# The last 64 tokens' mixing of a token mixer, written as products on half of TensorE's array

## The chip, the cores and the metric

The kernel runs on one core of a Trainium2 chip. The metric is the device time of one execution in microseconds; three executions of the kernel before gave 269.45, 269.69 and 269.77 us, a median of 269.69. The engines are called TensorE (PE in the profile, with PEld for its weight loads), VectorE (DVE), ScalarE (ACT), GpSimd (POOL) and SyncE (SP, which issues most of the transfers here).

## The reference

Eight batches; each is a linear attention of 8 heads over 576 tokens with head size 64, followed by an MLP mixer over 512 features. Written per batch:

```
phi(x)  = concat(relu(x) * cos_w, relu(x) * sin_w)      # [576, 128] per head
kv      = phi(k)^T @ v            ; z = sum over tokens of phi(k)
x       = (phi(q) @ kv) / (phi(q) @ z + 1e-6)           # heads side by side: [576, 512]
h       = relu(x^T @ w_tok1) @ w_tok2                   # token mixing: 576 -> 256 -> 576
u       = x + h^T
out     = u + relu(u @ w_ch1) @ w_ch2                   # channel mixing: 512 -> 1536 -> 512
```

Inputs and outputs are float32; the products take bfloat16 operands and add up in float32.

## The kernel before, in words

576 tokens are 4 x 128 + 64. The 512 "main" tokens of a batch are cut into four chunks of 128 (R = 4 chunks; chunk number ci is 0 to 3), and the last 64 tokens are a fifth chunk, numbered R. Two batches, an even one and the odd one after it, share the tiles of the last tokens: the even batch has partitions 0 to 63 and the odd one 64 to 127 (`half(0)` and `half(1)`; `self.rows` is the batch's own half). So the features of q and k, their transposes and the channel mixing of the last tokens are worked for two batches at once.

The token mixing of the last tokens is not shared. It runs once per batch on whole-array products in which half of the rows or half of the results go to nothing:

- `num` (L353 to L371) makes one chunk of x: 8 products, one per head, of 65 columns (64 values and the denominator), then a reciprocal and a multiplication on VectorE. For chunk R the stationary operand is the shared transposed q of both batches, so 128 result rows come out, and VectorE keeps only the batch's own 64 of them. x of the last tokens is kept in a tile of 128 rows whose other half was cleared to zero once at the start (L162 to L164).
- `tok1` (L373 to L383) is the first token mixing, 576 tokens to 256: for each of the two blocks of 128 hidden tokens (mi) it adds up five products of 512 columns, one per chunk, in the order `ORDER = (0, 1, 2, R, 3)`. For chunk R the weights stand in both halves of `w_tail1`, and the zero rows of x make the other half add nothing. `tok1_out` (L385) applies relu and stores B1.
- `tok2` (L391 to L413) is the second token mixing, 256 to 576: two products of 512 columns per chunk (ki), an addition of x on VectorE that gives u, and a cast on ScalarE. For chunk R the weights' 64 columns stand twice, so that the result comes out on both halves, and VectorE adds x on the batch's own 64 rows only.

After that, u is transposed by a DMA (for chunk R once per pair), and the channel mixing (`Channel`, L532 to L634) runs: `c_main` 12 x 4 products of 512 columns, `o_step` 12 products of 512 columns per chunk, and in odd batches the same for the shared last tokens.

The order of all this is written out by hand. The program of each batch's channel mixing is a list of steps (`Channel.steps`), and the preparation of the next batch, from features to token mixing, is put behind numbered steps of it by the table in `Front.pieces` (L461 to L527). There, C counts from the first c step and O from the first o step; `(t + at, T, ci)` places the second token mixing, `mix` the first, `N` the numerators. A batch's token mixing thus falls between the o steps of the batch before. The lines of that table that place the mixing:

```python
plan += [(mix, self.mix_head, 0), (mix + 1, self.mix_head, 1),
         (mix + 2, self.mix_tail)]
plan += [(t + at, T, ci) for ci, at in enumerate((0, 1, 2, 3, 3) if not first else
                                                 (0, 0, 1, 2, 2))]
```

`mix_head` does chunks 0, 1, 2 and R of one block, `mix_tail` chunk 3 and the relu. The first batch has no batch before it and is prepared by `first_front` (L636 to L712), in which the denominators are made separately (`dens`, L295); its u of chunk R is made at step 10 of its own channel mixing and cast at step O + 8 (L477, L483).

SyncE's queue holds the loads of q, k and v, the transposing DMAs and the stores; POOL's queue holds the weight loads (L182 to L198).

Of the kernel before, what the change touches and what calls it, by code (L numbers as in the profile page):

```python
# [9 lines left out]
F32 = mybir.dt.float32  # L10
BF16 = mybir.dt.bfloat16
# [5 lines left out]
def kernel(  # L17
# [15 lines left out]
    nc = tc.nc  # L33

    B, H, S, D = q.shape
    F = 2 * D
    Dm = H * D
    S_tok, D_tok = moe_w_tok1.shape
    Dm2, D_ch = moe_w_ch1.shape
    P = 128  # L40
    R = S // P
    SM = R * P
    ST = S - SM
    NSC = R + 1
    NCC = Dm // P
    NT = D_tok // P
    NCH = D_ch // P
    HH = H // 2
    D1 = D + 1
    DP = 80  # L50
# [2 lines left out]


    ORDER = (0, 1, 2, R, 3)

    def half(g):
        return slice(g * ST, (g + 1) * ST)
# [7 lines left out]
    twos = ctx.enter_context(tc.tile_pool(name="twos", bufs=2))  # L66
    o_out = ctx.enter_context(tc.tile_pool(name="o_out", bufs=4))
    phi = ctx.enter_context(tc.tile_pool(name="phi", bufs=R))
    once = ctx.enter_context(tc.tile_pool(name="once", bufs=1))
    const = ctx.enter_context(tc.tile_pool(name="const", bufs=1))  # L70
    small = ctx.enter_context(tc.tile_pool(name="small", bufs=4))
    ps_mm = ctx.enter_context(tc.tile_pool(name="ps_mm", bufs=4, space=bass.MemoryType.PSUM))
# [44 lines left out]
    w_tok2n = stage2[:, 0:NT * S].rearrange("p (n s) -> p n s", n=NT)  # L117
# [7 lines left out]
    w_ch2 = const.tile([P, NCH, Dm], BF16, name="w_ch2")  # L125
    w_tok1 = const.tile([P, R, D_tok], BF16, name="w_tok1")

    w_tail1 = const.tile([P, D_tok], BF16, name="w_tail1")
    w_tok2 = const.tile([P, NT, SM + P], BF16, name="w_tok2")
    ident = head.tile([P, P], BF16, name="ident")  # L130
    make_identity(nc, ident)
    pos_i = head.tile([P, NSC], mybir.dt.int32, name="pos_i")
# [19 lines left out]
    nc.gpsimd.memset(ones[half(1), 1:2], 0.0)  # L152


    v_augs, x_tails = [], []
    for i in range(2):
        va = const.tile([P, NSC, H, DP], BF16, name=f"v_aug{i}")
        nc.vector.memset(va[:, 0:R, :, D:D1], 1.0)
        nc.vector.memset(va[half(1 - i), R, :, :], 0.0)
        nc.vector.memset(va[half(i), R, :, D:D1], 1.0)  # L160
        v_augs.append(va)
        xt = const.tile([P, Dm], BF16, name=f"x_tail{i}")  # L162
        nc.vector.memset(xt[half(1 - i), :], 0.0)
        x_tails.append(xt)  # L164

    class Tail:

# [12 lines left out]
    for t in (tail0.kp, tail0.qp):  # L180
        nc.gpsimd.memset(t[half(1)], 0.0)
    for g in range(2):  # L182
        nc.gpsimd.dma_start(out=w_tail1[half(g), :], in_=moe_w_tok1[SM:S, :])
    C2 = D_ch // 2
    w_ch1_done = []
    for c2 in range(2):
        for ki in range(0, NCC, 2):
            w_ch1_done.append(nc.gpsimd.dma_start(
                out=w_ch1[:, ki:ki + 2, c2 * C2:(c2 + 1) * C2],
                in_=moe_w_ch1[ki * P:(ki + 2) * P, c2 * C2:(c2 + 1) * C2]  # L190
# [18 lines left out]
    def permute_tok2(ki):  # L209
        nc.scalar.copy(w_tok2[:, ki, 0:SM].rearrange("t (r p) -> t r p", r=R),  # L210
                       w_tok2n[:, ki, 0:SM].rearrange("t (p r) -> t r p", r=R))
        nc.scalar.copy(w_tok2[:, ki, SM:].rearrange("t (g s) -> t g s", g=2),
                       w_tok2n[:, ki, None, SM:S].to_broadcast([P, 2, ST]))


    class Front:
# [17 lines left out]
        def q_of(self, ci):  # L234
            return self.qp[ci] if ci < R else self.tail.qp

        def qT_of(self, ci, h):
            return self.qpT[:, ci * H + h, :] if ci < R else self.tail.qpT[:, h, :]

        def x_of(self, ci):  # L240
            return self.x[:, ci, :] if ci < R else self.xt

        def rows_of(self, ci):
            return slice(0, P) if ci < R else self.rows

        def feature(self, which, ci, j, heads=(0, H), on_act=False):
            lo, hi = heads
# [18 lines left out]
        def values(self, ci, eng, heads=(0, H)):  # L266
            lo, hi = heads
            if ci < R:
                src = self.vt[:, lo:hi, ci * D:(ci + 1) * D]
            else:  # L270
                src = self.tail.vt[self.rows, lo:hi, :]
            dst = self.va[self.rows_of(ci), ci, lo:hi, 0:D]
            if eng is nc.scalar:
                nc.scalar.copy(dst, src)  # L274
            else:
                eng.tensor_copy(dst, src)
# [18 lines left out]
        def dens(self, ci):  # L295

            if ci == 0:
                self.d_ps = ps_mm.tile([P, NSC * H], F32, name="d_ps", tag="mm")
                self.d_sb = small.tile([P, NSC * H, 1], F32, name="d_sb")
            for h in range(H):  # L300
                i = ci * H + h
                nc.tensor.matmul(self.d_ps[:, i:i + 1], self.qT_of(ci, h),  # L302
                                 self.ks_sb[:, h:h + 1], start=True, stop=True)

        def dens_out(self, lo, hi):
            nc.vector.tensor_scalar_add(self.d_sb[:, lo:hi, 0], self.d_ps[:, lo:hi], 1e-6)
# [46 lines left out]
        def num(self, ci, fill=0, dens=False):  # L353
            num_ps = ps_at.tile([P, 2, 512], F32, name="num_ps", tag="at")
            if fill:
                busy(num_ps[:, 0, HH * DP:512], 1)
            for h in range(H):
                g, j = divmod(h, HH)
                nc.tensor.matmul(num_ps[:, g, j * DP:j * DP + D1], self.qT_of(ci, h),  # L359
                                 self.kv_sb[g][:, j, 0:D1], start=True, stop=True)  # L360
            rows = self.rows_of(ci)
            nv = num_ps[rows, :, 0:HH * DP].rearrange("p g (j d) -> p g j d", d=DP)
            if dens:
                den = self.d_sb[rows, ci * H:(ci + 1) * H, :].rearrange("p (g j) o -> p g j o", g=2)
            else:
                den = small.tile([P, 2, HH, 1], F32, name="den")[rows]
                nc.vector.tensor_scalar_add(den, nv[:, :, :, D:D1], 1e-6)
                nc.vector.reciprocal(den, den)
            nc.vector.tensor_mul(  # L369
                self.x_of(ci)[rows].rearrange("p (g j d) -> p g j d", g=2, j=HH),  # L370
                nv[:, :, :, 0:D], den.to_broadcast([rows.stop - rows.start, 2, HH, D]))  # L371

        def tok1(self, mi, chunks):  # L373
            if not hasattr(self, "B1"):
                self.B1 = once.tile([P, NT, Dm], BF16, name="B1")
                self.b1_ps = {}
            if mi not in self.b1_ps:
                self.b1_ps[mi] = ps_mm.tile([P, Dm], F32, name="b1_ps", tag="mm")
            cols = slice(mi * P, (mi + 1) * P)
            for ci in chunks:  # L380
                w = w_tok1[:, ci, cols] if ci < R else w_tail1[:, cols]
                nc.tensor.matmul(self.b1_ps[mi], w, self.x_of(ci),  # L382
                                 start=(ci == ORDER[0]), stop=(ci == ORDER[-1]))  # L383

        def tok1_out(self, mi, on_act=True):  # L385
            if on_act:
# [2 lines left out]
                nc.vector.tensor_relu(self.B1[:, mi, :], self.b1_ps[mi])  # L389

        def tok2(self, ci, pool=None, turn=True):  # L391
            res, tail = self.res, self.tail
            if ci == 0:
                res["u"] = keep.tile([P, R, Dm], F32, name="u_sb")
                if turn:
                    self.new_uT()
                    self.ub = once.tile([P, R, Dm], BF16, name="u_bf")
            if ci == R and not hasattr(tail, "u"):
                tail.new_u()
            if pool is None:  # L400
                u_ps = ps_mm.tile([P, Dm], F32, name="u_ps", tag="mm")
            else:
                u_ps = pool.tile([P, Dm], F32, name="u_ps", tag="at")
            rows = self.rows_of(ci)
            for ki in range(NT):
                nc.tensor.matmul(u_ps, w_tok2[:, ki, ci * P:(ci + 1) * P],  # L406
                                 self.B1[:, ki, :], start=(ki == 0), stop=(ki == NT - 1))
            u = res["u"][:, ci, :] if ci < R else tail.u[rows]
            nc.vector.tensor_add(u, u_ps[rows], self.x_of(ci)[rows])  # L409
            if turn and ci == R:  # L410
                self.tail_cast()
            elif turn:
                nc.scalar.copy(self.ub[:, ci, :], u)  # L413

        def tail_cast(self):
            nc.scalar.copy(self.tail.ub[self.rows], self.tail.u[self.rows])

        def new_uT(self):

# [31 lines left out]
            self.feature("q", ci, 1, on_act=on_act)  # L451

        def mix_head(self, mi):
            self.tok1(mi, ORDER[:-1])

        def mix_tail(self):
            for mi in range(NT):
# [3 lines left out]
        def pieces(self, b, before):  # L461
# [6 lines left out]
            C, O = 0, NCH  # L468
            if first:
# [4 lines left out]
                        (8, V, 2, pool), (8, load_w_ch2, 0), (8, V, 3, pool),  # L474
                        (8, load_w_ch2, 1), (8, load_w_ch2, 2),
                        (8, u, 2, None, False), (9, V, 1, act), (9, u, 3, None, False),
                        (9, QS, 0), (10, u, R, None, False)]  # L477
                plan += [(11, KV, ci) for ci in range(NSC)]
                plan += [(11, QS, 1), (11, QS, 2), (11, self.kv_out),
                         (11, QT, 0, (0, H), act, ps_at), (11, QT, 1), (11, QS, R),  # L480
                         (O, QT, 2), (O, N, 0), (O, QS, 3), (O + 1, QT, R),
                         (O + 1, N, 1), (O + 3, N, 2), (O + 3, QT, 3),
                         (O + 5, N, R), (O + 7, N, 3), (O + 8, before.tail_cast)]  # L483
            else:
                plan = [(C + at, V, ci, nc.scalar)
                        for ci, at in enumerate((6, 6, 7, 7, 7) if late else (-1, -1, 0, 1, 2))]
# [25 lines left out]
            else:  # L512
# [2 lines left out]
            plan += [(mix, self.mix_head, 0), (mix + 1, self.mix_head, 1),  # L515
                     (mix + 2, self.mix_tail)]

            plan += [(t + at, T, ci) for ci, at in enumerate((0, 1, 2, 3, 3) if not first else
                                                             (0, 0, 1, 2, 2))]
            plan += [(t + 3 - first, self.u_trans_dma, 3, R)]  # L520
            plan.append((t + 2 - first, self.u_trans_dma, 0, 3))
            if odd:
# [113 lines left out]
    def first_front(f):  # L636
# [54 lines left out]
        for i, ci in enumerate(ORDER):  # L691
            if i + 2 < NSC:
                f.num(ORDER[i + 2], dens=True)
            for mi in range(NT):
                f.tok1(mi, (ci,))
        for mi in range(NT):
# [113 lines left out]
```

## Time and profile before

| | |
|---|---|
| median of three runs | 269.69 us (269.45 to 269.77) |
| the profiled execution | 269.69 us |
| its span, first to last instruction | 267.9 us |
| TensorE busy | 261.1 us, 2050 products |
| weight loads (beside the products) | 139.5 us, 2050 loads |
| VectorE / ScalarE / GpSimd busy | 164.5 / 129.6 / 14.5 us |
| first mixing, last tokens (L382, x_tail) | 16 products of 512 columns |
| second mixing (L406), all chunks | 80 products of 512 columns, 16 of them for the last tokens |
| numerators, last tokens (L359, qpT_tail) | 64 products of 65 columns |
| transfers | 53.68 MB, 200 GB/s on average |

Busy time of TensorE in the profile counts a product from its start to its modelled end (379 ns for 512 columns), and products overlap; how long one occupies the engine is read from the distance of two starts. The span is cut into 40 equal slices, in each of which a digit gives the busy tenths of an engine. The chain that ended last is followed back from the last instruction: at each step to what released it, or to the instruction before it on its engine.

### The profile page before, as it was taken

How to read it: one execution, taken by the hardware profiler on the slowest of the kernel's cores; microseconds unless marked ns; L12 is line 12 of the kernel's file. 1: busy time of each engine (PE TensorE's matmuls, PEld its weight loads, DVE VectorE, ACT ScalarE, POOL GpSimd, SP SyncE). 2: the span in 40 equal slices, each digit the busy share in tenths (PEclk: the TensorE clock that was granted, in tenths of full speed). 3: DMA queues.
4: the chain of work that ended last, by engine and by line, in shares of the span. 5: the costliest groups of instructions: out<-in, count | busy, mean ns of one | idle time of the engine just before them, and what ended most of it. 6: DMA issues, size and time to landing. Idle time of an engine off the chain costs nothing.

```text
span 267.9 us, 5123 instructions
## 1 busy us (share of the span) xinstructions
PE 261.1 (97%) x2050; PEld 139.5 (52%) x2050; DVE 164.5 (61%) x376; ACT 129.6 (48%) x228; POOL 14.5 (5%) x24
## 2 busy tenths in 40 slices
PE   7989999999999999999999999999999999999994
PEld 2665466455644455446644455446644455445543
DVE  5965798784566846876565846876565846820022
ACT  3982876428606362546516362547515362526400
POOL 6450230000000000000000000000000000000000
PEclk9999999999999999999999999999999999999999
DMA  7999999679999999469974999199974580170032
GB/s 222 359 232 270 350 175 274 225 198 290 166 340 282 273 176 346 124 166 273 209 265 117 289 223 348 59 183 239 238 253 117 157 120 0 57 200 1 2 109 87
DMA packets 91815, 53.68 MB, mean 200 GB/s; under 512 B 59408, under 2 KB 86928, under 8 KB 91792
## 3 DMA queue, kind: packets, MB, share of 16 engines
q1 hardware_dynamic: 88432, 49.62, 69.7%
q0 software_dynamic: 2832, 3.21, 7.6%
q10 hardware_dynamic: 528, 0.52, 0.6%
q8 instruction: 16, 0.26, 0.4%
q14 instruction: 7, 0.06, 0.1%
HBM read 35.85 MB, written 9.44 MB: 169 GB/s over the span
## 4 chain that ended last, share of the span: by engine, by line
PE 92%; DVE 3%; ACT 2%; DMA 2%; issue 0%; DVEq 0%; ACTq 0%
PE o_ps L579 35%; PE c_ps L546 29%; PE u_ps L406 6%; PE b_ps L382 6%; PE num_ps L359 4%; PE ct_ps L566 4%; PE kv_ps L320 3%; DMA qt<-in_q_dram 2%; DVE qp L263 1%; PE idle_ps L204 1%; PE qT_ps L340 1%; ACT v_aug L274 1%; PE c_ps L556 1%; ACT h1T L550 1%; PE t_ps L433 1%; PE d_ps L302 0%
## 5 line engine op out<-in xcount | busy, mean ns | idle before, releaser
L579 PE MATMUL o_ps<-w_ch,h1T 128*128 128x512 bf16 (+1 forms) x396 | 94.1, 372 | 0.0
L546 PE MATMUL c_ps<-uT,w_ch 128*128 128x512 bf16 (+2 forms) x384 | 92.2, 372 | 0.1
L550 ACT ACTIVATE h1T<-c_ps 128x512 bf16<-128x512 f32 x93 | 55.4, 598 | 59.9 <-PE c_ps L546 59.5
L579 PEld LDWEIGHTS <-h1T 128*128 128x128 bf16 x396 | 37.3, 98 | 39.5 <-issue 0.2
L546 PEld LDWEIGHTS <-w_ch 128*128 128x128 bf16 x384 | 33.5, 97 | 29.6 <-issue 0.2
L584 DVE TENSOR_TENSOR o_sb<-o_ps,u_sb 128x512 f32<-128x512 f32 (+1 forms) x33 | 22.3, 674 | 29.5 <-PE o_ps L579 29.4
L409 DVE TENSOR_TENSOR u_sb<-u_ps,x_sb 128x512 f32<-128x512 f32 x32 | 21.7, 689 | 6.0 <-PE u_ps L406 5.6
L413 ACT CAST u_bf<-u_sb 128x512 bf16<-128x512 f32 x28 | 17.3, 619 | 16.7 <-DVE u_sb L409 16.7
L406 PE MATMUL u_ps<-B,w_tok 128*128 128x512 bf16 x80 | 22.6, 379 | 0.0
L387 ACT ACTIVATE B<-b_ps 128x512 bf16<-128x512 f32 x8 | 4.8, 597 | 35.4 <-PE b_ps L382 35.4
L369 DVE TENSOR_TENSOR x_sb<-num_ps,den 128x512 bf16<-128x512 f32 x28 | 19.4, 692 | 1.0
L566 PEld LDWEIGHTS <-w_ch 128*128 128x128 bf16 x192 | 14.0, 98 | 9.2
L382 PE MATMUL b_ps<-x_sb,w_tok 128*128 128x512 bf16 x64 | 17.9, 379 | 0.0
L566 PE MATMUL ct_ps<-uT_tail,w_ch 128*128 128x128 bf16 x192 | 17.2, 219 | 0.0
L263 DVE TENSOR_SCALAR kp<-kt,cos_t 128x512 bf16<-128x512 f32 x32 | 15.1, 478 | 3.1 <-DMA kt<-in_k_dram 3.1
L274 ACT CAST v_aug<-vt 128x512 bf16<-128x512 f32 (+1 forms) x30 | 16.7, 586 | 0.1
L263 DVE TENSOR_SCALAR qp<-qt,cos_t 128x512 bf16<-128x512 f32 (+1 forms) x35 | 15.9, 453 | 1.0 <-DMA qt<-in_q_dram 1.0
L263 DVE TENSOR_SCALAR qp<-qt,sin_t 128x512 bf16<-128x512 f32 (+1 forms) x35 | 15.9, 453 | 0.0
L584 DVE TENSOR_TENSOR o_sb<-o_ps,u_tail 128x512 f32<-128x512 f32 x4 | 2.8, 692 | 19.0 <-PE o_ps L579 19.0
L359 PEld LDWEIGHTS <-qpT 128*128 128x128 bf16 x256 | 11.5, 98 | 5.5 <-issue 1.3
L359 PE MATMUL num_ps<-kv_sb,qpT 128*128 128x65 bf16 x256 | 13.0, 193 | 0.9 <-DVE x_sb L369 0.5
L331 DVE CAST kv_sb<-kv_ps 128x260 bf16<-128x260 f32 x8 | 3.5, 433 | 16.6 <-ACT kv_sb L331 16.5
(93 smaller groups left out, 233.4 us busy)
## 6 DMA issues: line engine op xcount, KB each, us to landing
out_dram<-o_sb SPq DMA_DIRECT2D x31, 256.0 KB, 2.9
kt<-in_k_dram SPq DMA_DIRECT2D x7, 1024.0 KB, 6.7
vt<-in_v_dram SPq DMA_DIRECT2D x7, 1024.0 KB, 6.5
qt<-in_q_dram SPq DMA_DIRECT2D x7, 1024.0 KB, 8.3
w_ch<-in_moe_w_ch_dram POOLq DMA_DIRECT2D x4, 384.0 KB, 8.3
w_ch<-in_moe_w_ch_dram POOLq DMA_DIRECT2D x3, 512.0 KB, 7.5
out_dram<-o_sb SPq DMA_DIRECT2D x10, 128.0 KB, 2.3
qtt<-in_q_dram SPq DMA_DIRECT2D x8, 128.0 KB, 5.6
```

The lines of the kernel that those rows point to most:

```text
L263: nc.vector.tensor_scalar(o_ap, i_ap, scalar1=w, scalar2=0.0, op0=ALU.mult, op1=ALU.max)
L274: nc.scalar.copy(dst, src)
L359: nc.tensor.matmul(num_ps[:, g, j * DP:j * DP + D1], self.qT_of(ci, h), self.kv_sb[g][:, j, 0:D1], start=True, stop=True)
L369: nc.vector.tensor_mul(self.x_of(ci)[rows].rearrange("p (g j d) -> p g j d", g=2, j=HH), nv[:, :, :, 0:D], den.to_broadcast([rows.stop - r ...
L382: nc.tensor.matmul(self.b1_ps[mi], w, self.x_of(ci), start=(ci == ORDER[0]), stop=(ci == ORDER[-1]))
L406: nc.tensor.matmul(u_ps, w_tok2[:, ki, ci * P:(ci + 1) * P], self.B1[:, ki, :], start=(ki == 0), stop=(ki == NT - 1))
L409: nc.vector.tensor_add(u, u_ps[rows], self.x_of(ci)[rows])
L546: nc.tensor.matmul(c_ps[:, lo:hi], w_ch1[:, ki, mi * P:(mi + 1) * P], uT[:, lo // P:hi // P, ki, :], start=(ki == 0), stop=(ki == NCC - 1))
L550: nc.scalar.activation(self.h1T[:, mi, :], c_ps, AF.Relu)
L566: nc.tensor.matmul(self.ct_ps[:, mi % R, :], w_ch1[:, ki, mi * P:(mi + 1) * P], self.tail.uT[:, ki, :], start=(mi % R == 0 and ki == 0), s ...
L579: nc.tensor.matmul(o_ps, h, w_ch2[:, ki, cols], start=ki == 0, stop=ki == NCH - 1)
L584: nc.vector.tensor_add(o_sb, o_ps, u)
```

## The change

The last tokens' mixing is rewritten so that no product computes results or adds rows that are thrown away.

- Numerators (and the first batch's denominators) of chunk R: per head two products instead of one, each with only the batch's own 64 columns of the transposed q as the stationary operand. One writes result rows 0 to 63, the other the same values to rows 64 to 127. So x of the last tokens stands twice, in both halves, and the zeroed half goes.
- First mixing of chunk R (`tok1_last`): one product per block as before, but on 64 rows: block 0 takes rows 0 to 63 of x and of the weights, block 1 takes rows 64 to 127. `w_tail1` holds block 0's weights in its upper half and block 1's in its lower half. Both are issued together after the second block's chunks 0 to 2.
- Second mixing of chunk R (`tok2_last`): once per pair, in the odd batch's place in the table. Four products of 512 columns, each with 64 stationary columns: for each ki one for the even batch into result rows 0 to 63 and one for the odd batch into rows 64 to 127. Two additions on VectorE and one cast of all 128 rows on ScalarE follow. B1 of the even batch has to live until then, so B1 gets two buffers.

```diff
+    MAIN = tuple(ci for ci in ORDER if ci < R)
...
-    w_tail1 = const.tile([P, D_tok], BF16, name="w_tail1")
-    w_tok2 = const.tile([P, NT, SM + P], BF16, name="w_tok2")
+    w_tail1 = const.tile([P, P], BF16, name="w_tail1")
+    w_tok2 = const.tile([P, NT, S], BF16, name="w_tok2")
...
-        xt = const.tile([P, Dm], BF16, name=f"x_tail{i}")
-        nc.vector.memset(xt[half(1 - i), :], 0.0)
-        x_tails.append(xt)
+        x_tails.append(const.tile([P, Dm], BF16, name=f"x_tail{i}"))
...
     for g in range(2):
-        nc.gpsimd.dma_start(out=w_tail1[half(g), :], in_=moe_w_tok1[SM:S, :])
+        nc.gpsimd.dma_start(out=w_tail1[half(g), :],
+                            in_=moe_w_tok1[SM:S, g * P:(g + 1) * P])
...
-        nc.scalar.copy(w_tok2[:, ki, SM:].rearrange("t (g s) -> t g s", g=2),
-                       w_tok2n[:, ki, None, SM:S].to_broadcast([P, 2, ST]))
+        nc.scalar.copy(w_tok2[:, ki, SM:S], w_tok2n[:, ki, SM:S])
...
-        def qT_of(self, ci, h):
-            return self.qpT[:, ci * H + h, :] if ci < R else self.tail.qpT[:, h, :]
+        def by_query(self, ci, h, dst, moving):
+            if ci < R:
+                nc.tensor.matmul(dst, self.qpT[:, ci * H + h, :], moving, start=True, stop=True)
+                return
+            for g in range(2):
+                nc.tensor.matmul(dst[half(g)], self.tail.qpT[:, h, self.rows], moving,
+                                 start=True, stop=True)
...
-                nc.tensor.matmul(self.d_ps[:, i:i + 1], self.qT_of(ci, h),
-                                 self.ks_sb[:, h:h + 1], start=True, stop=True)
+                self.by_query(ci, h, self.d_ps[:, i:i + 1], self.ks_sb[:, h:h + 1])
...
-                nc.tensor.matmul(num_ps[:, g, j * DP:j * DP + D1], self.qT_of(ci, h),
-                                 self.kv_sb[g][:, j, 0:D1], start=True, stop=True)
-            rows = self.rows_of(ci)
-            nv = num_ps[rows, :, 0:HH * DP].rearrange("p g (j d) -> p g j d", d=DP)
+                self.by_query(ci, h, num_ps[:, g, j * DP:j * DP + D1],
+                              self.kv_sb[g][:, j, 0:D1])
+            nv = num_ps[:, :, 0:HH * DP].rearrange("p g (j d) -> p g j d", d=DP)
...
-                self.B1 = once.tile([P, NT, Dm], BF16, name="B1")
+                self.B1 = twos.tile([P, NT, Dm], BF16, name="B1")
...
-            cols = slice(mi * P, (mi + 1) * P)
             for ci in chunks:
-                w = w_tok1[:, ci, cols] if ci < R else w_tail1[:, cols]
-                nc.tensor.matmul(self.b1_ps[mi], w, self.x_of(ci),
+                nc.tensor.matmul(self.b1_ps[mi], w_tok1[:, ci, mi * P:(mi + 1) * P], self.x_of(ci),
                                  start=(ci == ORDER[0]), stop=(ci == ORDER[-1]))
+
+        def tok1_last(self):
+            for mi in range(NT):
+                nc.tensor.matmul(self.b1_ps[mi], w_tail1[half(mi), :], self.xt[half(mi), :],
+                                 start=False, stop=False)
...
-            if ci == R and not hasattr(tail, "u"):
-                tail.new_u()
...
-            u = res["u"][:, ci, :] if ci < R else tail.u[rows]
-            nc.vector.tensor_add(u, u_ps[rows], self.x_of(ci)[rows])
-            if turn and ci == R:
-                self.tail_cast()
-            elif turn:
+            u = res["u"][:, ci, :]
+            nc.vector.tensor_add(u, u_ps, self.x_of(ci))
+            if turn:
                 nc.scalar.copy(self.ub[:, ci, :], u)
 
-        def tail_cast(self):
-            nc.scalar.copy(self.tail.ub[self.rows], self.tail.u[self.rows])
+        def tok2_last(self, before):
+            tail = self.tail
+            tail.new_u()
+            u_ps = ps_mm.tile([P, Dm], F32, name="u_ps", tag="mm")
+            for ki in range(NT):
+                for g, f in enumerate((before, self)):
+                    nc.tensor.matmul(u_ps[half(g), :], w_tok2[:, ki, SM:S], f.B1[:, ki, :],
+                                     start=(ki == 0), stop=(ki == NT - 1))
+            for g, f in enumerate((before, self)):
+                nc.vector.tensor_add(tail.u[half(g)], u_ps[half(g)], f.xt[half(g)])
+            nc.scalar.copy(tail.ub, tail.u)
...
         def mix_head(self, mi):
-            self.tok1(mi, ORDER[:-1])
+            self.tok1(mi, MAIN[:-1])
+            if mi == NT - 1:
+                self.tok1_last()
...
-                        (9, QS, 0), (10, u, R, None, False)]
+                        (9, QS, 0)]
...
-                         (O + 5, N, R), (O + 7, N, 3), (O + 8, before.tail_cast)]
+                         (O + 5, N, R), (O + 7, N, 3)]
...
-            plan += [(t + at, T, ci) for ci, at in enumerate((0, 1, 2, 3, 3) if not first else
-                                                             (0, 0, 1, 2, 2))]
+            plan += [(t + at, T, ci) for ci, at in enumerate((0, 1, 2, 3) if not first else
+                                                             (0, 0, 1, 2))]
+            if odd:
+                plan.append((t + 3 - first, self.tok2_last, before))
...
+            if ci == R:
+                f.tok1_last()
+                continue
             for mi in range(NT):
                 f.tok1(mi, (ci,))
```

More of the change, by code (lines that the diff above doesn't have):

```diff
@@ L235, in q_of @@
             return self.qp[ci] if ci < R else self.tail.qp
-        def qT_of(self, ci, h):
-            return self.qpT[:, ci * H + h, :] if ci < R else self.tail.qpT[:, h, :]
+        def by_query(self, ci, h, dst, moving):
[5 more added lines that the diff above has]
+                                 start=True, stop=True)
         def x_of(self, ci):
             return self.x[:, ci, :] if ci < R else self.xt
-        def rows_of(self, ci):
-            return slice(0, P) if ci < R else self.rows
         def feature(self, which, ci, j, heads=(0, H), on_act=False):
@@ L271, in values @@
                 src = self.tail.vt[self.rows, lo:hi, :]
-            dst = self.va[self.rows_of(ci), ci, lo:hi, 0:D]
+            dst = self.va[slice(0, P) if ci < R else self.rows, ci, lo:hi, 0:D]
             if eng is nc.scalar:
@@ L358, in num @@
                 g, j = divmod(h, HH)
-                nc.tensor.matmul(num_ps[:, g, j * DP:j * DP + D1], self.qT_of(ci, h),
-                                 self.kv_sb[g][:, j, 0:D1], start=True, stop=True)
-            rows = self.rows_of(ci)
-            nv = num_ps[rows, :, 0:HH * DP].rearrange("p g (j d) -> p g j d", d=DP)
+                self.by_query(ci, h, num_ps[:, g, j * DP:j * DP + D1],
+                              self.kv_sb[g][:, j, 0:D1])
+            nv = num_ps[:, :, 0:HH * DP].rearrange("p g (j d) -> p g j d", d=DP)
             if dens:
-                den = self.d_sb[rows, ci * H:(ci + 1) * H, :].rearrange("p (g j) o -> p g j o", g=2)
+                den = self.d_sb[:, ci * H:(ci + 1) * H, :].rearrange("p (g j) o -> p g j o", g=2)
             else:
-                den = small.tile([P, 2, HH, 1], F32, name="den")[rows]
+                den = small.tile([P, 2, HH, 1], F32, name="den")
                 nc.vector.tensor_scalar_add(den, nv[:, :, :, D:D1], 1e-6)
                 nc.vector.reciprocal(den, den)
-            nc.vector.tensor_mul(
-                self.x_of(ci)[rows].rearrange("p (g j d) -> p g j d", g=2, j=HH),
-                nv[:, :, :, 0:D], den.to_broadcast([rows.stop - rows.start, 2, HH, D]))
+            nc.vector.tensor_mul(self.x_of(ci).rearrange("p (g j d) -> p g j d", g=2, j=HH),
+                                 nv[:, :, :, 0:D], den.to_broadcast([P, 2, HH, D]))
         def tok1(self, mi, chunks):
             if not hasattr(self, "B1"):
-                self.B1 = once.tile([P, NT, Dm], BF16, name="B1")
+                self.B1 = twos.tile([P, NT, Dm], BF16, name="B1")
                 self.b1_ps = {}
@@ L391, in tok2 @@
         def tok2(self, ci, pool=None, turn=True):
-            res, tail = self.res, self.tail
+            res = self.res
             if ci == 0:
@@ L403, in tok2 @@
                 u_ps = pool.tile([P, Dm], F32, name="u_ps", tag="at")
-            rows = self.rows_of(ci)
             for ki in range(NT):
```

## The prediction

> **What bounds the kernel now.** I read the busy shares and the slices of the span first, then the chain that ended last, then the costliest groups, and last TensorE's own timeline around the steps that change.
>
> ```profile
> span 267.9 us, 5123 instructions
> PE 261.1 (97%) x2050; PEld 139.5 (52%) x2050; DVE 164.5 (61%) x376; ACT 129.6 (48%) x228; POOL 14.5 (5%) x24
> PE   7989999999999999999999999999999999999994
> PEclk9999999999999999999999999999999999999999
> PE 92%; DVE 3%; ACT 2%; DMA 2%; issue 0%; DVEq 0%; ACTq 0%
> ```
>
> TensorE is busy in every slice but the first and the last, its granted clock is whole throughout, and 92% of the chain is TensorE. A busy share alone could hide gaps, so I checked the pace in the timeline, whose first columns are start and length of a group; the next group's start minus its own, divided by the count, is the time that one product occupies the engine.
>
> ```profile
> 39.18 0.59 PE L579 MATMUL o_ps<-w_ch,h1T 128*128 128x512 bf16 x2
> 39.61 0.61 PE L340 MATMUL qT_ps<-ident,qp 128*128 128x128 bf16 x8
> 40.06 0.41 PE L359 MATMUL num_ps<-kv_sb,qpT 128*128 128x65 bf16 x8
> 40.30 0.59 PE L579 MATMUL o_ps<-w_ch,h1T 128*128 128x512 bf16 x2
> ...
> 102.44 0.41 PE L359 MATMUL num_ps<-kv_sb,qpT_tail 128*128 128x65 bf16 x8
> 102.69 1.46 PE L579 MATMUL o_ps<-w_ch,h1T 128*128 128x512 bf16 x6
> 103.98 0.41 PE L359 MATMUL num_ps<-kv_sb,qpT 128*128 128x65 bf16 x8
> ```
>
> Six products of 512 columns take 102.69 to 103.98, 0.216 us each; eight of 65 columns take 0.24 us, 30 ns each; eight transposes take 0.45 us, 56 ns each. Group follows group at exactly these paces, also where a 512-column product is followed by a transpose or a 65-column one: no gap between kinds. The list of waits has TensorE waiting for another engine some 3 us in all, 1.4 of it for the identity in the start-up. So from about 20 us on the time is the sum of what TensorE issues, and each nanosecond of TensorE's time that the change adds or removes moves the end.
>
> ```profile
> L406 PE MATMUL u_ps<-B,w_tok 128*128 128x512 bf16 x80 | 22.6, 379 | 0.0
> L382 PE MATMUL b_ps<-x_tail,w_tail 128*128 128x512 bf16 x16 | 5.9, 379 | 0.0
> L359 PE MATMUL num_ps<-kv_sb,qpT_tail 128*128 128x65 bf16 x64 | 3.3, 193 | 0.0
> L302 PE MATMUL d_ps<-ks_sb,qpT_tail 128*128 128x1 bf16 x8 | 0.3, 164 | 0.0
> L416 ACT CAST ub_tail<-u_tail 64x512 bf16<-64x512 f32 x8 | 4.9, 617 | 0.5
> ```
>
> These are the groups that change. All are 128*128 forms: no product on half an array is in this trace, so what a half costs has to be bounded. One product's record (379 ns) is 163 ns longer than its share of the engine (216), the time in which its results are still on the way while the next one streams.
>
> **The change part by part.** The sum stands against the profiled execution: 269.69 us, span 267.9 and 1.8 around it; the median of the three runs is the same 269.69.
>
> *First mixing, last tokens.* Before: two 512-column products in each of 8 batches, 16 x 0.216 = 3.46 us. After: the two of a batch use the upper and the lower 64 rows and write different banks. Side by side, a pair costs one stream plus the issue of the second. The nearest row for that issue is the pace of one-column products, whose stream is nothing:
>
> ```profile
> 10.54 0.46 PEld L340 LDWEIGHTS <-qp_tail 128*128 128x128 bf16 x8 [0.47 <-issue]
> 10.57 0.61 PE L340 MATMUL qT_ps<-ident,qp_tail 128*128 128x128 bf16 x8 [0.17 <-DVE qp_tail L263]
> ...
> 15.00 0.74 PE L302 MATMUL d_ps<-ks_sb,qpT 128*128 128x1 bf16 x24
> 15.60 0.59 PE L320 MATMUL kv_ps<-v_aug,kp 128*128 128x65 bf16 x14
> ```
>
> 24 of them in 0.60 us, 25 ns each. Saved: 8 x (216 - 25) = 1.53 us. Ends: 8 x 216 = 1.73 us if the second is free, 0 if halves run one after the other.
> By the Trainium skill, "TensorE: Matmul & The Clock Gate", part 3 on packing small products, several tiles of the array were measured running at once (four row tiles 3.07 times as fast, three column tiles 2.38 times). Nothing in this trace shows it; by two thirds to three quarters of the ideal gain, as there, the two mixings together would give 2.3 to 2.7 us.
>
> *Second mixing, last tokens.* Before: two products per batch, 3.46 us. After: four half-column products per pair of batches, two at a time, so again 8 pairs instead of 16 products: 1.53 us, same ends. I take side by side, since both operands of the two halves lie in different partitions or columns; together 3.06 us are saved.
>
> *The numerators of the last tokens.* Before: 8 products of 65 columns per batch; after: 16, each with 64 stationary columns, because x is wanted in both halves. Low end: the second of each pair rides along, nothing added. High end: each of the 16 pays its weight load bare; the lines above show the first product 0.03 us after its load on an idle engine, so 0.03 + 0.03 each, 16 x 0.06 - 0.24 = 0.7 us a batch, 5.8 in all. I take 16 at the 30 ns of the same stream length: +0.24 a batch, +1.9 us. The first batch's denominators grow by 8 one-column products, 8 x 25 ns = 0.2 us.
>
> *Changing between whole and half array.* There are 8 groups of numerators, 1 of denominators, 8 of first mixing and 4 of second: 21 groups, each entered from and left to whole-array products, 42 changes. Low end of the price: 0, by the gapless change between transposes and products above. High end: the products in flight must be out, 163 ns, then a load stands bare, 28 ns: 191 ns. The value I take is an estimate from rows: a column takes 216/512 = 0.42 ns per step, so passing 128 rows takes 54 ns, plus the 25 ns at which loads follow each other: 79 ns, 42 x 0.079 = 3.3 us. It lies between the two ends; the transposes show that a change of operation is free, but they keep the same rows and columns, so I do not take zero.
> The Trainium skill, "TensorEngine Tiling (Array Packing)", key properties, says that changing the tiling mode, unlike changing the tile, drains TensorE, and it speaks against this change. It has no figure; by its rule with the whole 163 ns the changes would cost some 8 us, without it nothing, and no row of this trace decides.
>
> *Beside the path.* Eight casts of 64 rows (617 ns) become four of 128 rows (the 128-row casts of the same width take 619): ScalarE is 2.5 us less busy, at 48%. VectorE keeps eight additions of 64 rows; in odd batches two follow each other (2 x 0.68 us), so the last tokens' cast and transposing DMA of SP start about 0.7 us later, some 6 us of output steps ahead of the first product that reads them; if that cover were gone it would cost 0.7 us four times. The numerator's scaling takes 690 ns on 64 rows and 692 on 128. First-batch last tokens no longer mix early; their two products move behind the second batch's, with the cast at one slot instead of two. Two clears of x (0.27 us each) go from the start, where VectorE waits for q anyway. Half as much weight is loaded on POOL's queue for the last tokens, two DMAs as before. B1's second buffer takes away a wait that no view shows. I cost these at nothing. No wait is added: the x and B1 of the even batch are there one batch (some 30 us) before the odd batch's slot reads them. The bounds of the bookkeeping are -0.5 and +0.7 us.
>
> *Sum:* -3.06 + 1.9 + 0.2 + 3.3 = +2.3 us, 272.0 us.
>
> **The rivals.**
> - *The change of division is free* (or hidden in the 163 ns that overlap anyway). For it: no gap between kinds of product in this trace. Against: none of those kinds splits the array. Then -3.06 + 2.1 = -1.0, 268.7 us, and down to 266.8 if the numerators pair up as well. It decides below 23 ns a change (the point where -1.0 is eaten up), or below some 69 if the numerators pair. This is the one on the other side: faster.
> - *The engine empties whole at each change.* 42 x 191 ns = 8.0 us instead of 3.3: 276.7 us. For it: the 163 ns tail of every record; against: part of that tail may be reading of operands, which can go on ahead.
> - *Halves run one after the other*, so that the change does not do what it says. The 3.06 us go: 275.1 us with the price of changes as taken, 271.8 without. For it: only that nothing here shows overlap between products.
> - *Half-width loads set the pace of the numerators.* Bare loads, 0.06 us a product: 3.9 us more than taken, 275.9 us. For it: a load's record is 98 ns against a pace of 30, so three overlap today, and two halves of a column division may not. Against: a half-width load has half the columns.
> The Trainium skill's "TensorEngine Tiling (Array Packing)", restrictions, says that column tiling switches off fast weight load; with the load time of "TensorE: Matmul & The Clock Gate" (columns over 1.2 ns) an estimate is 53 ns a product and 275 us. No row here shows a load without it.
>
> **How the numbers follow.** Forecast 0.34 (changes of 30 to 130 ns, 270 to 274 us); free change 0.30; whole emptying 0.13; halves in turn 0.11; slow loads 0.12. A measurement of this kernel tells some 0.2% (0.54 us) from no change. Faster: the free change nearly whole, 0.29; same: the seam between it and the forecast, 0.09; slower: the rest, 0.62. The range goes from 267.2 (free change with part of the pairing) to 276.8 (whole emptying); about 0.07 lies below and 0.1 above, where two of the slow rivals meet. The forecast alone has 270 to 274.
>
> **What the changed profile would show.** Side by side: the two half products of a pair start some 25 ns apart and the next whole product about 216 ns later; in turn: 216 apart. The price of a change: the start of the first product of another division minus the last start before it, less that product's own stream; 79 ns by the forecast, nothing by the first rival, 190 by the second. Numerators: 16 starts at 30 ns, or 60 by the rival on loads. TensorE should stay the chain's 90% and more; a new wait of it for the last tokens' transposing DMA would upset the bookkeeping. I am wrong if the groups of the last tokens become shorter by what is saved without gaps around them.

## The result, and the profile after

The changed kernel takes 270.99 us (median of six; 270.88 to 271.35), the kernel before 269.58 in the same comparison: a ratio of 1.0052, with a 95% interval of 1.004 to 1.0065. It is slower, by 1.41 us at the medians. The profiled execution took 270.95 us, with a span of 268.8. Against the profiled execution before (269.69 us, span 267.9), 0.9 us of the loss lies in the span and 0.35 around it (2.15 us now, 1.8 before).

From the page of the changed kernel, the span, the busy shares, the clock and the chain:

```profile
span 268.8 us, 5231 instructions
PE 261.0 (97%) x2098; PEld 137.3 (51%) x2122; DVE 164.5 (61%) x374; ACT 126.7 (47%) x224; POOL 10.9 (4%) x24
PEclk9999999999999999999999999999999999999999
PE 95%; ACT 2%; issue 1%; DVE 1%; POOL 0%; POOLq 0%; ACTq 0%
```

TensorE still is the chain. There are 72 weight loads more than the 2050 of before (64 for numerators, 8 for denominators); 24 records of products are missing from this trace, so the loads are what to count. Its timeline shows the three places (start, length, group; L242 are the half numerators, L385 and L420 the two half mixings):

```profile
102.48 0.44 PE L242 MATMUL num_ps<-kv_sb,qpT_tail 128*64 128x65 bf16 x16
102.85 1.47 PE L591 MATMUL o_ps<-w_ch,h1T 128*128 128x512 bf16 x5
...
105.91 0.81 PE L379 MATMUL b_ps<-x_sb,w_tok 128*128 128x512 bf16 x3
106.66 0.39 PE L385 MATMUL b_ps<-x_tail,w_tail 64*128 64x512 bf16 x2
106.98 0.61 PE L591 MATMUL o_ps<-w_ch,h1T 128*128 128x512 bf16 x2
...
111.33 0.59 PE L406 MATMUL u_ps<-B,w_tok 128*128 128x512 bf16 x2
111.86 0.62 PE L420 MATMUL u_ps<-B,w_tok 128*64 128x512 bf16 x4
```

Two products on row halves last 0.39 us together, hardly longer than one alone (0.379): they run side by side. But three whole products before them take 0.75 us from start to next start (105.91 to 106.66) where 3 x 0.216 = 0.65 is due, and the pair takes 0.32 (106.66 to 106.98) where one stream is 0.216: some 0.1 us is lost going in and 0.1 coming out. The weight loads, on their own row of the same timeline, say how:

```profile
106.13 0.10 PEld L379 LDWEIGHTS <-w_tok 128*128 128x128 bf16 x1
106.65 0.10 PEld L385 LDWEIGHTS <-w_tail 64*128 64x128 bf16 x2 [0.42 <-issue]
106.66 0.39 PE L385 MATMUL b_ps<-x_tail,w_tail 64*128 64x512 bf16 x2
106.97 0.11 PEld L591 LDWEIGHTS <-h1T 128*128 128x128 bf16 x2 [0.23 <-issue]
```

Between whole products the next load stands beside the running product. At a change of division it is not issued until 307 ns after the last product's start (106.345 to 106.652, single records), 91 ns after that product's stream has ended, and the new product starts 4 ns behind it. From the starts of single products:

| | start to start, ns | of that the product's own share | price |
|---|---|---|---|
| whole, 512 columns, to a column half | 309 | 216 | 93 |
| whole, 512 columns, to a row half | 311 to 312 | 216 | 96 |
| column half, 65 columns, to whole | 125 to 129 | 29 | 96 to 100 |
| column half, 512 columns, to whole | 311 (three of four lack the next record) | 216 | 95 |
| row half, 512 columns, to whole | 318 to 320 (the first batch's 414 holds a wait for x) | 216 | 103 |
| second half of a pair behind the first | 2 to 9 | | |

The table misses a small part of the price: the first whole 512-column product after such a group holds the engine for 225 to 227 ns instead of 216, so some 10 ns more belong to each return.

### The profile page after: what moved, and what is told of

It is laid out like the page before. It is cut to its first block, busy times and chain, and to the rows that moved or that the text cites. A ratio compares the mean times of both kernels' runs of the same rounds, so it can differ in the third digit from the quotient of the medians.

```text
span 268.8 us, 5231 instructions
## 1 busy us (share of the span) xinstructions
PE 261.0 (97%) x2098; PEld 137.3 (51%) x2122; DVE 164.5 (61%) x374; ACT 126.7 (47%) x224; POOL 10.9 (4%) x24
## 4 chain that ended last, share of the span: by engine, by line
PE 95%; ACT 2%; issue 1%; DVE 1%; POOL 0%; POOLq 0%; ACTq 0%
PE o_ps L591 35%; PE c_ps L558 29%; PE u_ps L406 5%; PE b_ps L379 5%; PE idle_ps L205 4%; PE ct_ps L578 4%; PE kv_ps L321 3%; PE num_ps L239 3%; PE qT_ps L341 2%; PE num_ps L242 1%; PE b_ps L385 1%; PE c_ps L568 1%; ACT v_aug L276 1%; ACT h1T L562 1%; PE u_ps L420 1%
## 5 line engine op out<-in xcount | busy, mean ns | idle before, releaser
L591 PE MATMUL o_ps<-w_ch,h1T 128*128 128x512 bf16 (+1 forms) x380 | 92.2, 373 | 0.9 <-issue 0.5
L591 PEld LDWEIGHTS <-h1T 128*128 128x128 bf16 x396 | 36.3, 98 | 40.5 <-issue 3.5
L406 PE MATMUL u_ps<-B,w_tok 128*128 128x512 bf16 x62 | 18.7, 379 | 0.2
L239 PEld LDWEIGHTS <-qpT 128*128 128x128 bf16 x288 | 12.6, 98 | 5.9 <-issue 1.3
```

The source lines that it names most:

```text
L239: nc.tensor.matmul(dst, self.qpT[:, ci * H + h, :], moving, start=True, stop=True)
L406: nc.tensor.matmul(u_ps, w_tok2[:, ki, ci * P:(ci + 1) * P], self.B1[:, ki, :], start=(ki == 0), stop=(ki == NT - 1))
L591: nc.tensor.matmul(o_ps, h, w_ch2[:, ki, cols], start=ki == 0, stop=ki == NCH - 1)
```

## The experiments

Stages are compared by the start of the first weight load of each batch's channel mixing, in which the token mixing of the next batch is placed; how much longer than in the kernel before each stretch got, in ns, from the profiled executions (batches counted from 0 in this table):

| mixing in the stretch | changed kernel | second alone (again) | x whole | numerators alone | first alone |
|---|---|---|---|---|---|
| batch 4 (even) | -198 | -431 | -440 | +232 | -2 |
| batch 5 (odd) | +458 | +225 | +228 | +234 | +1 |
| batch 6 (even) | -199 | -432 | -442 | +234 | -5 |
| batch 7 (odd) | +460 | +224 | +227 | +235 | -4 |

**The second mixing alone.**

```diff
+            for ki in range(NT):
+                for g, f in enumerate((before, self)):
+                    nc.tensor.matmul(u_ps[half(g), :], w_tok2[:, ki, SM:S], f.B1[:, ki, :], ...)
```

> The kernel before with the second mixing's part of the change alone (last tokens of a pair in column halves); numerators and first mixing stay whole. Theory A, each change between whole and half array costs about 98 ns (93 to 103 in the trace of the changed kernel) and the halves run side by side: per pair four whole products (864 ns) go, 460 ns of half products and two changes (about 200 ns) come, so 4 x -0.20 = -0.8 us, about 268.8 us, faster by 0.3%. Rival B, changes of division cost nothing to speak of and the loss sits elsewhere (numerators, bookkeeping): 4 x -0.40 = -1.6 us, about 268.0. Rival C, the moved additions and the single cast delay something: no gain, 269.6 or more.

> The second mixing's part alone once more, on the same chip as the variant with the earlier load. Theory A: 0.8 us less than before in the steady part, 268.8 us; with the wait for w_ch2 of its first profile up to 1.1 us of it is lost again. Every pair of batches from the third batch on should again be 0.20 us shorter.

Measured: 269.37 us, ratio 0.9974 (0.9953 to 0.9994); again on another occasion 268.75 us, ratio 0.9942 (0.9926 to 0.9957). In the steady stretches a pair of batches is 206 ns shorter (-431 + 225), as theory A has it; B's 400 is out, and so is C. The whole times decide less: the same kernel gained 0.26% on one occasion and 0.58% (at least 0.43%, 1.2 us) on the other, where theory A has 0.3%, and no view explains the surplus. From the timeline of the second profile, where two whole products, the group of four halves and the next whole products start:

```profile
110.94 0.59 PE L402 MATMUL u_ps<-B,w_tok 128*128 128x512 bf16 x2
111.46 0.62 PE L415 MATMUL u_ps<-B,w_tok 128*64 128x512 bf16 x4
112.02 2.33 PE L584 MATMUL o_ps<-w_ch,h1T 128*128 128x512 bf16 x10
```

0.52 us for two whole products instead of 0.43: the price of entering again. The four halves take 0.56 us, 0.1 more than their own 0.46: the price of leaving. The profiled execution of the first occasion had this wait of TensorE in the first batch, from its list of waits:

```profile
PE o_ps L584 <- DMA w_ch<-in_moe_w_ch_dram: 1.1, 2, 0.8
```

The profile of the second occasion did not have it. That this wait made the first gain the smaller one is not shown, and the run with the earlier load below does not bear it out.

**Numerators alone.** Before, with 16 half products per batch and zero weights in `w_tail1`'s lower half.

> The kernel before with the numerators' and denominators' part alone (16 half products instead of 8, x twice); the first mixing stays whole, with zero weights in the lower half, and the second stays as it was. Theory A: 8 x 0.22 + 0.23 = +2.0 us, about 271.6 us. Rival B: +0.3 us, about 269.9.

Measured: 271.92 us, ratio 1.0079 (1.0057 to 1.0102), +2.1 us by the ratio; 232 to 235 ns in every batch, even and odd. Theory A, and the table accounts for it: 93 ns to enter, 100 to leave, 10 at the return and 30 of products are 233. The numerators in column halves alone cost more than the whole change loses.

**x twice by whole products.** The changed kernel, with the last tokens' transposed q stored twice side by side. The shared tile that it is copied from (`qpT_tail`) also goes from two buffers to one, here and in the variant after this one.

```diff
-            for g in range(2):
-                nc.tensor.matmul(dst[half(g)], self.tail.qpT[:, h, self.rows], moving, ...)
+            nc.tensor.matmul(dst, self.qpT2[:, h, :], moving, start=True, stop=True)
...
+        def q_twice(self):
+            self.twice(self.tail.qpT, nc.gpsimd.tensor_copy)
```

> The changed kernel, but x of the last tokens gets into both halves by whole-array products: the own 64 columns of the transposed q are copied twice side by side (by GpSimd, for the first two batches by ScalarE), so the 9 column-half groups of numerators and denominators go and 8 products instead of 16 stay. Theory A: each numerator group cost two changes and 30 ns, the denominators 0.23, so 8 x 0.22 + 0.23 = 2.0 us less than the changed kernel, about 269.0 us, 0.2% faster than before. Rival B (changes are free): the numerators' own products cost only 0.03 us a batch more than before, so about 0.3 us less than the changed kernel, 270.7.

Measured: 270.27 us, ratio 1.0018 (0.9995 to 1.0041). In the steady stretches a pair is now 214 ns shorter than before, 474 less than the changed kernel: 237 a batch, theory A's size. But the whole gained only about 0.9 us (1.0052 to 1.0018) of the 2.0 expected. A part is a new wait, from the list of waits of this kernel:

```profile
PEld L242 <- POOL qpT L352: 1.6, 1, 1.6
PE num_ps L242 <- POOL qpT L352: 1.1, 1, 1.1
```

It falls once, on the third batch, whose q arrives late by the table and whose copy on GpSimd is not done in time.

**First mixing alone.** The same whole-array x, row halves for the first mixing, the second as before.

> The kernel before with the first mixing's part alone (row halves), x twice by whole-array products as in the run above, second mixing whole as before. Theory A: per batch the second product saves 212 ns and two changes cost 199, so 8 x -0.013 = -0.1 us, about 269.5, not to be told from no change. Rival B: 8 x -0.21 = -1.7 us, about 267.9.

Measured: 270.94 us, ratio 1.0044 (1.0022 to 1.0065), so neither expectation for the whole held. The stretches do decide between the theories: -2, +1, -5, -4 ns, the break-even of theory A, where B would have had -210. The profile is of the slowest of the twelve executions (272.39 us). All of the loss in its span lies ahead of the third batch's channel mixing, which starts 2.4 us late; there the profile lists waits for GpSimd's copy and 0.6 us for w_ch2. Another 0.3 us lies around the span, as in every kernel here without the clears. How much of the loss is the variant's own copying or its single buffer was not separated.

**One product more behind each numerator group**, whole, on a column half, on a column half and a row half, or on both column halves.

```diff
+            nc.tensor.matmul(num_ps[half(0), 0, HH * DP:HH * DP + 1], ident[:, half(0)], zeros[:, 0:1],
+                             start=True, stop=True)
```

> The kernel before with one extra one-column whole-array product behind each of the 40 groups of numerators (into an unused column, its result is not read). Control for the next three. Both theories: one-column products follow each other at 25 ns, 40 x 0.025 = +1.0 us, about 270.7 us.

> As the control, but the extra product is on a column half (64 stationary columns). Theory A (a change of division costs about 98 ns each way whatever runs before or after): 40 x (97 to enter + 102 to the next start) = +8.0 us, about 277.6 us, 7 us above the control. Theory B (the prices read in the trace belong to the long products or the pairs there): between +1 and +4 us.

> As the control, but two extra products, the first on a column half, the second on a row half. Theory A1, any change of division costs its 98 ns: three changes, 40 x 0.30 = +12 us, about 281.6 us. Theory A2, only entering and leaving the whole array costs, half to half is free: +8.1 us, about 277.7 us.

> As the control, but two extra products, one on each column half. Theory A: the second starts 3 to 4 ns behind the first, so +8.0 to +8.2 us, about 277.7 us, as with one. Rival: each tile pays for itself, then +12 us or more.

Measured against 270.13 us of the kernel before: whole 270.81 (ratio 1.0026, 1.0009 to 1.0043); column half 278.18 (1.0298, 1.0268 to 1.0328); column and row half 282.71 (1.0466, 1.0433 to 1.05); both column halves 278.50 (1.0311, 1.028 to 1.0343). The column half costs 8.05 us over the kernel before and 7.4 over the control; the other column half adds 0.3 us; going on to a row half adds 4.5 us. The steady stretches, with five groups each, give the price of one group without the scatter of whole runs: 26 ns for the whole product, 227 for the column half (201 over the control), 230 for both column halves and 333 for column and row half (107 more than the column half alone). So the price is the change of division, in every direction tried and with streams of 1, 65 and 512 columns, and not the half product or the changed position within one division. Theories A and A1 hold, A1 with 1.1 us more than its 281.6; A2, B and the rival of the last run fall. From the timeline of the kernel with both kinds:

```profile
103.36 0.41 PE L359 MATMUL num_ps<-kv_sb,qpT 128*128 128x65 bf16 x8
103.70 0.19 PE L361 MATMUL num_ps<-zeros,ident 128*64 128x1 bf16 x1
103.82 0.17 PE L363 MATMUL num_ps<-zeros,ident 64*128 64x1 bf16 x1
103.93 1.04 PE L550 MATMUL c_ps<-uT,w_ch 128*128 128x512 bf16 x4
```

Each one-column product holds the engine for 0.11 to 0.12 us, against 25 ns in whole-array streams, and the eight numerators before them take 0.34 instead of 0.24.

**The clears of x kept.** The changed kernel with L162 to L164 of before.

> The changed kernel with the two clears of x's other halves kept at the start (they are overwritten later). In the profiles 1.7 to 1.8 us lie around the span of the kernel before and of the second mixing alone, but 2.1 to 2.2 around that of the changed kernel and of the three variants without the clears. Theory M, the missing clears go with these 0.35 us: 1.8 us around the span and about 270.6 us. Rival N, something else of the change: 2.1 us around the span, 271.0 us as before.

Measured: 270.59 us, ratio 1.0026 (1.0009 to 1.0042), and 1.77 to 1.90 us around the span in all twelve executions, against 2.09 to 2.18 in all six of the changed kernel. Span 268.8 as before the edit. Theory M. Whether it is the clears as such or only two more instructions on VectorE, no run tells.

**An earlier load of w_ch2**, on top of the second mixing alone.

```diff
+        if third == 0:
+            after(w_ch2_done[0], first_loads[1])
...
-                        (8, V, 2, pool), (8, load_w_ch2, 0), (8, V, 3, pool),
+                        (8, load_w_ch2, 0), (8, V, 2, pool), (8, V, 3, pool),
```

> The kernel with the second mixing's part alone, and the first third of w_ch2 issued on GpSimd's queue ahead of the cast of the values of chunk 2 instead of behind it (still after the second batch's values have landed). In the profile of the second mixing alone TensorE waited 1.1 us for w_ch2 in the first batch, where the removed product pair of the first batch's last tokens had given it 0.43 us more. Theory D, that wait takes the missing part of the steady gain: the transfer starts 0.6 us earlier, so 0.5 us less than the second mixing alone, about 268.8 us and a profile with at most 0.5 us of that wait. Rival E, the landing is set by the other transfers on the same engines: no change, 269.3.

Measured: 269.44 us, ratio 0.9983 (0.9961 to 1.0006), beside 268.75 for the second mixing alone on the same occasion. The profile has no wait for w_ch2, but a new one:

```profile
PE num_ps L360 <- DMA qpT<-qp: 0.6, 1, 0.6
```

The wait that theory D named is gone and the gain did not come. The runs spread from 268.26 to 271.08, so whether the edit costs or the transfers fell badly stays open; it is no gain.

## Why the prediction was right

Slower was forecast with a chance of 0.62 and 272.0 us; 270.99 was measured, inside the range of 267.2 to 276.8 and inside the forecast case's own 270 to 274. The mechanism was the one put first: halves side by side, and a price for changing the division that eats the gain. That the sum came out within 1 us is in part luck: the numerators were put 1.7 us too high and the changes 0.8 us too low. With the numerators as measured and the rest as forecast, the sum would have been +0.7 us, hardly more than the 0.54 us that a measurement tells from no change. The terms:

- *First mixing* (1.53 us saved): 8 pairs whose second product starts 3 to 4 ns behind, 8 x 212 ns = 1.70. The 25 ns of issue taken from one-column products was too much: the pair's loads go out together, 3 ns apart.
- *Second mixing* (1.53 saved): starts 3, 237 and 3 ns apart and then a stream of 216, 459 ns for what took 864, so 4 x 405 ns = 1.62.
- *Numerators* (+1.9): this is the term that was mis-sized. Not 16 products at 30 ns in turn but 8 pairs at about 30 ns; the group lasts 246 ns from its first start to its last, and with the last pair's own 29 ns 275; before, eight products held the engine for 245 ns. That is 30 ns a batch, +0.24 us in all, near the low end that the text had named. I took the row of the same stream length without letting the overlap, which I had assumed for the mixings, hold here too. Denominators with their two changes: about 0.2.
- *Changes of division* (42 x 79 ns = 3.3 us): 93 to 103 ns in the trace, 42 x 98 = 4.1 us. The estimate was a fifth too low. That the price is built as the estimate has it, of passing 128 rows and one load, no run shows: leaving products on 64 rows costs no less (103 ns) than leaving ones on 128 rows (95 to 100). With the denominators' products the sum in the span is -1.70 - 1.62 + 0.24 + 0.06 + 4.1 = +1.1 us, and +1.3 with 10 ns for each of the 21 returns; the profile has +0.9. The steady stretches fit: two numerator groups at 233 ns, 206 saved by the second mixing and nothing by the first are 260 ns a pair of batches, and 260 is measured (-198 + 458). The difference lies earlier: 0.2 us ahead of the first channel mixing and 0.15 in the stretch that mixes the third batch; why, no view shows.
- *Beside the path* (nothing, with bounds of -0.5 and +0.7): ScalarE, VectorE and the transposing DMA stayed hidden, as said: TensorE's list of waits has none for the last tokens' cast or transposing DMA. The two clears were put at nothing because VectorE waits there anyway, and that step failed: leaving them out costs 0.35 us around the span, as the run with them kept shows. The cause is open.

The rivals: a free change (0.30) is refuted by the 93 to 103 ns and by the 40 inserted products. Whole emptying at 191 ns (0.13) was right that the next load is held back and wrong on the size: the load starts 72 ns before the previous record's modelled end, so the whole tail of 163 ns is not waited for. (The tail alone, without the load's 28 ns, makes 42 x 163 ns = 6.8 us; the prediction's "some 8 us" for it counts the load too.) Halves in turn (0.11) and slow loads (0.12) are refuted by starts 3 ns apart and by pairs at 30 ns; only the first load after entering shows, with 49 ns between the first two pairs.

Two rules cited in the prediction can now be set beside numbers. The Trainium skill, "TensorEngine Tiling (Array Packing)", key properties: a change of tiling mode drains TensorE, a change of tile does not. This case agrees, at 93 to 103 ns for the one and 3 to 4 for the other. Its restrictions section, that column tiling goes without fast weight load, gave an estimate of 53 ns a product by "TensorE: Matmul & The Clock Gate"; half loads here last 106 to 113 ns in the records against 98 for whole ones, yet two run at once and the pairs keep a pace of some 30 ns, so that no such price appeared.

That the loss was a matter of how little each group saved for its two changes is shown by the second mixing alone: 405 ns saved for 200 of changes, and the kernel with this part alone is faster than the kernel before (0.9942 and 0.9974 of it) and so than the changed one. The first mixing saves 212 for 199 and is worth nothing; the numerators pay 200 and save nothing. Put together, -0.8 for the second mixing (4 x 206 ns) and nothing for the first, both from the steady stretches, and +2.1 for numerators and denominators (a whole run, also without the clears, so that the 0.35 around the span is in it) make +1.3 of the 1.41 us measured; the interval of the +2.1 alone is 1.5 to 2.7 us.

## What to carry to other kernels

Half-array products do run two at a time, at the price of one, but each group of them between whole-array products cost about 200 ns of TensorE here; a group paid when it removed two 512-column streams, broke even at one (212 ns), and lost where its products were short and none went. What follows from it, but was not tried here, is to bring all half products of one division together, so that they share two changes. Making the operand that is wanted twice by copies off TensorE did save 237 ns a batch, but one late copy cost 1.1 us of it: its arrival has to be covered. Before costing a removed instruction at nothing, look also at the time around the span.

## What the runs showed of the hardware that was not expected

- The price of a change of division depends little on what runs before or after: 92 ns to enter from 65-column products, 93 to 96 from 512-column ones, 95 to 100 to leave a column half, 103 to leave a row half of 512 columns, and half to half costs the same again (123 ns from start to start for a one-column product, of which 25 are its own). Lower prices are 81 ns to leave a one-column row half (106 from start to start) and 77 to leave the denominators (102). What these changes have in common is another distance: unless it waits for data or a record is missing, the new product starts 65 to 71 ns before the modelled end of the record ahead of it, in the changed kernel and in the runs with inserted products alike.
- Two clears of 64 x 512 elements on VectorE, at a time when VectorE waits for data (behind them it idles for 0.98 us in the kernel before), go with 0.35 us of device time outside the span: the profiled executions of all kernels with them had 1.7 to 1.8 us there, and those of the changed kernel and the three variants without them 2.1 to 2.2. The clears are not all of it: single other executions of the two kernels with two inserted products had 2.0 to 2.5 us there with the clears in place.
